# Smaller loads, full-height exponent products and another order of the first steps in a gated recurrence that feeds a mixture of experts

## The chip, the cores and the metric

The kernel runs on one core of a Trainium2 chip. The time is device microseconds of one execution; a kernel's time is the median of its runs. Five engines work side by side, each in the order of its own queue: PE (matrix products; PEld are its weight loads), VectorE (DVE), ScalarE (ACT), GpSimd (POOL) and SyncE (SP, which issues most transfers). [...]

## The reference

A recurrence over 768 positions for 4 batches and 8 heads of width 40, then a two-level choice of one of 16 experts for each of the 3072 tokens:

```python
for t in range(S):
    m_new = np.maximum(f_gate[:, :, t] + m, i_gate[:, :, t])
    f_stab = np.exp(f_gate[:, :, t] + m - m_new)
    i_stab = np.exp(i_gate[:, :, t] - m_new)
    C = f_stab * C + i_stab * np.einsum('bhd,bhe->bhde', vt, kt)
    n = f_stab * n + i_stab * kt
    h_tilde = np.einsum('bhde,bhe->bhd', C, qt)
    denom = np.maximum(np.abs(np.einsum('bhd,bhd->bh', n, qt)), 1.0)
    y[:, :, t] = sigmoid(o_gate[:, :, t]) * h_tilde / denom
x = y.transpose(0, 2, 1, 3).reshape(B * S, H * D)
...
g, e = best group of x, best expert in it
out = g_w * e_w * (relu(x @ w1[g, e]) @ w2[g, e])
```

## The kernel before

The positions are cut into 6 chunks of 128, each of two halves of 64 (`sub`); the batches into 2 groups of two (`bp`). A pair p is chunk c = p // 2 and group g = p % 2, so there are 12 pairs. Inside a chunk the recurrence is written as a masked product, between chunks as a carried state. The stages of a pair are functions:

- `load_qk`, `load_nt`: transfers of keys and queries (two of 320 KB, 40 rows each) and of keys, values and output gates in natural order (one of 968 KB, 128 rows of 7744 bytes). There are two `qk` buffers and three `nt` buffers.
- `exponents` (PE) adds up the exponents of the decays in PSUM: a mask, 16 products with the running sums `Z[:, 0]` and 8 with the sources `Z[:, 1]`, each for one half of the rows. `decays` (ACT) takes their exponential into `ab`. `Z` holds the sums of the gates split into three bf16 parts, one below the other.
- `scores` (PE) multiplies keys and queries, `masked` (DVE) multiplies scores and decays, `values` (PE) multiplies the result with the values.
- `keyw` (POOL) weights the keys, `state` (PE) forms the new state, `decayed` (POOL) and `added` (DVE) carry it on in `Cs`. `carried` (PE) is the queries' product with the carried state, in two groups; `carried2` (DVE) scales each group in `acc`.
- `gate` (ACT), `normed` (DVE) and `rows` (POOL) make the pair's output rows `x`; `store_rows` writes them to DRAM (`x_d`), `turn_rows` (PE transposes, ACT copies) turns them for `logits`, whose routing goes on as a chore.

`step(p)` writes down the work around pair p: values of p, exponents of p + 2, carried of p + 1, state and scores of p + 2. A chore is a list of small operations, mostly DVE's; `go_on(n)` issues n of them, and `STEPS` says how many at the four places of a step. The first chore, `far`, is the gates of chunks 2 to 5: five scans and sums on DVE (`gate_sums`), then the split (`parts`) on ACT and, before, POOL. `near` is the same for chunk 1. `gate_scales` makes the scale factors of a range of chunks.

The program is written under a manual schedule, so every engine's queue has the order of the code. The last products of `values` read a window of 64 columns that reaches into the gate columns of `nt`, so they wait for `gate` of the same pair. After the recurrence come 16 experts; their weights come through SP's queue too.

Of the kernel before, what the change touches and what calls it, by code (L numbers as in the profile page):

```python
# [66 lines left out]
def lstm_moe(ctx: ExitStack, tc: tile.TileContext, gates, qkT, nat, wcat, w1, w2, cst, out):  # L67
# [19 lines left out]
    ind_b, sel_b, hp_b = (cb[0:KP, a:b] for a, b in ((C_IND, C_SEL), (C_SEL, C_HP), (C_HP, C_LT)))  # L87
# [33 lines left out]
    Z = ap_.tile([KP, 2, S], BF16, name="Z")  # L121
    wk = att_pool("wk", 2)
# [49 lines left out]
    def exponents(p):  # L172
# [4 lines left out]
        for hp in range(2):  # L177
            for pr in range(4):
                for bp in range(2):
                    k = (2 * g + bp) * H + 4 * hp + pr  # L180
                    mm(t[SUB * bp:SUB * bp + SUB, hp, pr * P:(pr + 1) * P], bc(ind_b[:, k:k + 1], (KP, SUB)),
                       Z[:, 0, c * P:(c + 1) * P], start=False, stop=False, skip_group_check=True)
        for hp in range(2):
            for sub in range(2):
                for bp in range(2):
                    k = (2 * g + bp) * H + 4 * hp
                    at = c * P + sub * SUB
                    o = t[SUB * bp:SUB * bp + SUB, hp, :].rearrange("p (a s t) -> p a s t", a=4, s=2)[:, :, sub, :]
                    mm(o, Z[:, 1, at:at + SUB], bc(ind_b[:, k:k + 4].unsqueeze(2), (KP, 4, SUB)),  # L189
                       start=False, stop=(sub == 1), skip_group_check=True)  # L190
# [16 lines left out]
    def masked(p):  # L207
        pt = st_[p]["pt"] = wk.tile([P, 2 * H * SUB], F32, name="pt")
# [730 lines left out]
    STEPS = {8: (3, 5, 4, 5), 9: (6, 3, 2, 3), 10: (3, 5, 5, 6)}  # L939
# [19 lines left out]
    def step(p):  # L959
        n = STEPS.get(p) or (3, 4, 2, 3)  # L960
# [3 lines left out]
        run(values, p)  # L964
        run(normed, p)
        run(rows, p)
        if p > -2:
            run(load_nt, p + 3)
# [8 lines left out]
        if turned:  # L977
            logits()
# [418 lines left out]
```

## Time and profile before

| | us |
|---|---|
| median of 3 runs | 428.08 (420.79, 428.08, 431.43) |
| the profiled execution | 421.98 |
| its span | 420.3 |
| PE busy in the span | 374.1 (89%) |
| DVE, ACT, POOL busy | 296.7, 215.7, 134.1 |
| mean granted clock | 0.888 |

The span runs from the first to the last instruction; 1.7 us of the profiled execution lie outside it. Busy shares are means over stages with different limits, so the stages are read one by one below. "Idle before" is the time an engine stood still before an instruction, with what released it.

### The profile page before, as it was taken

To read this page: it belongs to the slowest core of one execution; us is meant where nothing else is said; L and a number is where in the kernel's file an instruction comes from. 1 tells how busy PE (TensorE), PEld (TensorE's weight loads), DVE (VectorE), ACT (ScalarE), POOL (GpSimd) and SP (SyncE) were. 2 spreads that over 40 slices of the span, in tenths; PEclk is the share of its full clock that TensorE was granted. 3 is DMA by queue.
4 is the path that set the end of the run, shared out by engine and by line. 5 is a ranking of instruction groups with operands and counts; after the bars stand their busy time and mean duration, and the time that the engine had idled before them with its cause. 6 is when DMAs were issued, how large, how long until landed. Compare 5 with 4: busy or idle time off the path is not lost.

```text
span 420.3 us, 12565 instructions
## 1 busy us (share of the span) xinstructions
PE 374.1 (89%) x5259; PEld 331.4 (79%) x5259; DVE 296.7 (71%) x695; ACT 215.7 (51%) x419; POOL 134.1 (32%) x143
## 2 busy tenths in 40 slices
PE   8497599779777867699999999999999999999994
PEld 4286377657666756696899999999999999999994
DVE  5457235766658755925788987987987779989893
ACT  2202523322313221445447776666777668888782
POOL 2234433433424233003252227314312343234121
PEclk9855656997969875689999999999999999999998
DMA  7735245674615773421587578568466865688200
GB/s 218 234 80 188 68 131 188 223 245 153 205 61 198 241 264 108 175 110 52 193 317 262 224 252 305 187 255 311 175 230 269 299 236 203 243 301 282 84 17 16
DMA packets 15772, 81.96 MB, mean 195 GB/s; under 512 B 2624, under 2 KB 6438, under 8 KB 11170
## 3 DMA queue, kind: packets, MB, share of 16 engines
q1 hardware_dynamic: 11890, 68.34, 47.3%
q0 software_dynamic: 3600, 12.39, 8.4%
q8 instruction: 42, 0.69, 0.7%
q10 hardware_dynamic: 224, 0.41, 0.3%
q14 instruction: 16, 0.13, 0.1%
HBM read 71.69 MB, written 9.93 MB: 194 GB/s over the span
## 4 chain that ended last, share of the span: by engine, by line
PE 66%; DVE 13%; issue 10%; DMA 4%; POOL 3%; ACT 3%; POOLq 1%; SPq 1%; DVEq 0%; ACTq 0%
PE psh L778 18%; PE po L828 5%; PE po L829 4%; PE po L830 4%; PE sp L204 4%; PE acc L289 4%; DMA nt<-in_nat_dram 4%; PE acc L265 4%; PE tp L332 3%; PE sp L230 3%; PE po L706 2%; PE psh L690 2%; PE po L834 2%; PE lg L353 2%; PE psh L803 2%
## 5 line engine op out<-in xcount | busy, mean ns | idle before, releaser
L608 POOL DMA_INDIRECT out_dram<-y,ix x32 | 36.7, 1146 | 112.9 <-ACT y L842 84.4
L778 PE MATMUL psh<-xhl,w1h 128*128 128x256 f32 (+4 forms) x336 | 58.5, 304 | 0.2
L828 PE MATMUL po<-w2h,hh 128*128 128x320 f32 (+1 forms) x176 | 55.6, 316 | 0.0
L830 PE MATMUL po<-w2h,hh 128*128 128x320 f32 (+1 forms) x176 | 54.4, 309 | 0.0
L829 PE MATMUL po<-w2l,hh 128*128 128x320 f32 (+1 forms) x176 | 54.3, 309 | 0.0
L749 DVE TENSOR_TENSOR w2l<-w2s,w2h 128x640 fp32r<-128x640 f32 x60 | 47.8, 823 | 6.4 <-ACT w2h L745 5.7
L778 PEld LDWEIGHTS psh<-xhl,w1h 128*128 128x128 f32 x336 | 49.8, 188 | 2.0 <-DVE xhl L811 0.6
L778 PE MATMUL psh<-xhl,w1l 128*128 128x128 f32 (+6 forms) x256 | 47.6, 268 | 0.0
L778 PE MATMUL psh<-xhl,wsk 128*128 128x256 f32 (+4 forms) x168 | 47.6, 322 | 0.0
L604 POOL DMA_INDIRECT xg<-x_d,ix x32 | 35.9, 1123 | 31.7 <-DVE hh L880 14.4
L778 PEld LDWEIGHTS psh<-xhl,w1l 128*128 128x128 f32 x256 | 42.3, 189 | 0.4
L749 DVE TENSOR_TENSOR w1l<-w1s,w1h 128x1024 fp32r<-128x1024 f32 x32 | 39.0, 1222 | 4.2 <-ACT w1h L745 4.0
L745 ACT CAST w2h<-w2s 128x640 fp32r<-128x640 f32 x60 | 41.5, 726 | 0.0
L194 ACT ACTIVATE ab<-sp 128x1024 f32<-128x1024 f32 x12 | 12.3, 1024 | 45.7 <-PE sp L189 34.7
L745 ACT CAST w1h<-w1s 128x1024 fp32r<-128x1024 f32 x32 | 33.3, 1046 | 0.0
L828 PEld LDWEIGHTS po<-w2h,hh 128*128 128x128 f32 (+1 forms) x176 | 32.6, 185 | 0.3
L830 PEld LDWEIGHTS po<-w2h,hh 128*128 128x128 f32 (+1 forms) x176 | 32.6, 185 | 0.2 <-DVE hh L880 0.2
L829 PEld LDWEIGHTS po<-w2l,hh 128*128 128x128 f32 (+1 forms) x176 | 32.6, 185 | 0.0
L265 PE MATMUL acc<-Cs,qk 40*64 40x64 f32 x704 | 21.6, 256 | 11.8 <-DVE acc L277 8.4
L334 ACT COPY xT<-tp 128x256 f32<-128x256 f32 x24 | 8.9, 373 | 45.0 <-PE tp L332 30.9
L265 PEld LDWEIGHTS acc<-Cs,qk 40*64 40x64 f32 x704 | 17.2, 163 | 16.1 <-DVE acc L277 9.7
L312 POOL TENSOR_TENSOR x<-sr,den 128x640 f32<-128x640 f32 (+1 forms) x12 | 15.4, 1283 | 44.9 <-DVE den L305 26.6
(208 smaller groups left out, 810.7 us busy)
## 6 DMA issues: line engine op xcount, KB each, us to landing
w1s<-in_w_dram SPq DMA_DIRECT2D x12, 1536.0 KB
w2s<-in_w_dram SPq DMA_DIRECT2D x14, 1280.0 KB
nt<-in_nat_dram SPq DMA_DIRECT2D x12, 968.0 KB
qk<-in_qkT_dram SPq DMA_DIRECT2D x24, 320.0 KB
x_d<-x SPq DMA_DIRECT2D x12, 384.0 KB
w1s<-in_w_dram SPq DMA_DIRECT2D x4, 768.0 KB
w1s<-in_w_dram POOLq DMA_DIRECT2D x2, 1536.0 KB, 7.4
w2s<-in_w_dram SPq DMA_DIRECT2D x4, 640.0 KB
```

What stands on the lines that cost most here:

```text
L204: mm(t[SUB * bp:SUB * bp + SUB, hp, pr * P + SUB * sub:pr * P + SUB * sub + SUB], qk[r, bp, 0, pr, s], qk[r, bp, 1, pr, s], start=True, st ...
L265: mm(acc[SUB * sub:SUB * sub + SUB, bp, 2 * pr + hp, :], qk[r, bp, 1, pr, SUB * sub:SUB * sub + SUB], Cs[r, at:at + WIN], start=(swap == 0 ...
L289: mm(acc[SUB * sub:SUB * sub + SUB, bp, j, :], pt[r, k:k + SUB], nt[r, v:v + WIN], start=(c == 0 and sub == 0 and j == 0), stop=(j == H - ...
L312: (e or nc.gpsimd).tensor_tensor(t["x"][:, bs, 0:DM].rearrange("p b (h d) -> p b h d", d=D), t["sr"][:, hs].rearrange("p (b h) d -> p b h ...
L604: return nc.gpsimd.indirect_dma_start(out=o, out_offset=None, in_=src, in_offset=bass.IndirectOffsetOnAxis(ap=idx, axis=0))
L608: return nc.gpsimd.indirect_dma_start(out=out, out_offset=bass.IndirectOffsetOnAxis(ap=idx, axis=0), in_=y, in_offset=None, bounds_check=N ...
L745: nc.scalar.copy(t[names[0]][:, dst], src[r][:, s])
L749: nc.vector.tensor_tensor(o, src[r][rows, s], h.bitcast(F32), op=ALU.subtract)
L778: mm(ps[:, g, 0:n_], w[:, s], x, start=(part == 0 and n == 0), stop=(part == 1 and n == len(todo[1]) - 1), skip_group_check=True)
L828: mm(po[0:m], hh[:, f, t], w2h[:, s], start=st0, stop=False)
L829: mm(po[0:m], hh[:, f, t], w2l[:, s], start=False, stop=False)
L830: mm(po[0:m], hh[:, f, tl], w2h[:, s], start=False, stop=sp0)
```

## The change

Four things change. A pair's `qk` load becomes 8 transfers (2 KB a row) and its `nt` load 6 (1296 or 1280 bytes a row). `exponents` uses full-height products: 8 with a table `ind2`, built once, and 4 with `zb`, the sources of both batches, which POOL's new stage `sources` makes a step ahead. `masked` writes over `ab`. And the order changes: pair 0's carried products, scales and `values` stand before pair 1's state, with 13 filler products (`busy`) between them; `keyw` of pair 1 stands behind `decayed` of pair 0; the chore `far` is spread over steps 0 and 1 behind the scalings, and its subtractions are on DVE; `turn_rows` of a pair's second half moves to the next step, between the two groups of `carried`, and `logits` behind `store_rows`.

```diff
@@ load_qk, load_nt
         for hp in range(2):
-            nc.sync.dma_start(qk[64 * hp:64 * hp + D], qkT[c, g, D * hp:D * hp + D])
+            for bp in range(2):
+                for i in range(2):
+                    nc.sync.dma_start(qk[64 * hp:64 * hp + D, bp, i], qkT[c, g, D * hp:D * hp + D, bp, i])
...
-        nc.sync.dma_start(nt, nat[c, g])
+        for a, b in ((0, NV // 2), (NV // 2, NV), (NV, NV + NV // 2), (NV + NV // 2, NTW), (NTW, NTW + DM), (NTW + DM, NTW + 2 * DM)):
+            nc.sync.dma_start(nt[:, a:b], nat[c, g, :, a:b])
@@ exponents
             for pr in range(4):
-                for bp in range(2):
-                    k = (2 * g + bp) * H + 4 * hp + pr
-                    mm(t[SUB * bp:SUB * bp + SUB, hp, pr * P:(pr + 1) * P], bc(ind_b[:, k:k + 1], (KP, SUB)),
-                       Z[:, 0, c * P:(c + 1) * P], start=False, stop=False, skip_group_check=True)
+                mm(t[:, hp, pr * P:(pr + 1) * P], ind2[:, g * H + 4 * hp + pr, :], Z[:, 0, c * P:(c + 1) * P],
+                   start=False, stop=False, skip_group_check=True)
         for hp in range(2):
             for sub in range(2):
-                for bp in range(2):
-                    k = (2 * g + bp) * H + 4 * hp
-                    at = c * P + sub * SUB
-                    o = t[SUB * bp:SUB * bp + SUB, hp, :].rearrange("p (a s t) -> p a s t", a=4, s=2)[:, :, sub, :]
-                    mm(o, Z[:, 1, at:at + SUB], bc(ind_b[:, k:k + 4].unsqueeze(2), (KP, 4, SUB)),
-                       start=False, stop=(sub == 1), skip_group_check=True)
+                o = t[:, hp, :].rearrange("p (a s t) -> p a s t", a=4, s=2)[:, :, sub, :]
+                mm(o, st_[p]["zb"][:, sub].rearrange("k b s -> k (b s)"), bc(hd_b[:, 4 * hp:4 * hp + 4].unsqueeze(2), (KP, 4, SUB)),
+                   start=False, stop=(sub == 1), skip_group_check=True)
+
+    def sources(p):
+        c, g = divmod(p, 2)
+        z = st_.setdefault(p, {})["zb"] = wk.tile([KP, 2, 2, SUB], BF16, name="zb")
+        nc.gpsimd.tensor_tensor(z, bc(Z[:, 1, c * P:(c + 1) * P].rearrange("k (s t) -> k s t", s=2).unsqueeze(2), (KP, 2, 2, SUB)),
+                                bc(b_b[:, 2 * g:2 * g + 2].unsqueeze(1).unsqueeze(3), (KP, 2, 2, SUB)), op=ALU.mult)
@@ masked
-        pt = st_[p]["pt"] = wk.tile([P, 2 * H * SUB], F32, name="pt")
+        pt = st_[p]["pt"] = st_[p]["ab"]
@@ step
-    STEPS = {8: (3, 5, 4, 5), 9: (6, 3, 2, 3), 10: (3, 5, 5, 6)}
+    STEPS = {0: (0, 3, 1, 1), 1: (0, 2, 1, 1), 8: (3, 4, 7, 6), 9: (6, 3, 2, 3), 10: (3, 5, 5, 6)}
...
-        n = STEPS.get(p) or (3, 4, 2, 3)
+        n = STEPS.get(p) or (3, 5, 3, 4)
...
         run(carried, p + 1, 0)
-        if turned:
-            logits()
+        if p > 0:
+            turn_rows(2 * p - 1)
         run(carried2, p + 1, 0)
...
+        listed()
+        store_rows(p)
+        run(load_qk, p + 3)
+        if turned:
+            logits()
+        turn_rows(2 * p)
...
-        if p >= 0:
-            turn_rows(2 * p + 1)
...
+        run(sources, p + 3)
@@ before the first step
-        near, far = gates_of(1, 2), gates_of(2, NCH, nc.scalar.copy, nc.gpsimd)
+        near, far = gates_of(1, 2), gates_of(2, NCH, nc.scalar.copy)
...
         steps(near, 2)
-        keyw(1)
+        spare = ps_1.tile([P, 4, P], F32, name="tp", tag="lg")
+        busy(4, spare)
         state(0)
         added(0, 0)
         decayed(0, 1)
+        keyw(1)
+        busy(3, spare)
         carried(0, 0)
+        busy(2, spare)
         carried2(0, 0)
-        steps(near, 2)
+        carried(0, 1)
+        busy(2, spare)
+        carried2(0, 1)
+        gate(0)
+        added(0, 1)
+        load_qk(2)
+        values(0)
+        busy(2, spare)
         state(1)
...
+        decayed(1, 1)
+        scores(1)
         steps(near, 99)
...
         for p in range(2):
-            step(p)
+            step(p, p == 0)
```

POOL's queue around pair 1's keys, before (`nt` with buffer numbers is the product `keyw`, `Cs` is `decayed`, `x` is `rows`, `Zr` the subtractions of `far`):

```order
L218 TENSOR_TENSOR nt_109<-nt_109,ab_107 128x2x320
L218 TENSOR_TENSOR nt_110<-nt_110,ab_108 128x2x320
L241 TENSOR_TENSOR Cs<-Cs,decs 128x328 x2
L312 TENSOR_TENSOR x<-sr,den 128x2x320
L218 TENSOR_TENSOR nt_111<-nt_111,ab_107 128x2x320
L241 TENSOR_TENSOR Cs<-Cs,decs 128x328
L1105 TENSOR_TENSOR Zr<-AC,Z 32x2x512
L1109 TENSOR_TENSOR Zr<-Zr,Zm 32x2x512
```

The same stretch of POOL's queue after:

```order
L194 TENSOR_TENSOR zb<-Z,cb 96x256 x2
L223 TENSOR_TENSOR nt_110<-nt_110,ab_108 128x2x320
L246 TENSOR_TENSOR Cs<-Cs,decs 128x328
L223 TENSOR_TENSOR nt_111<-nt_111,ab_109 128x2x320
L246 TENSOR_TENSOR Cs<-Cs,decs 128x328
L194 TENSOR_TENSOR zb<-Z,cb 96x256
L317 TENSOR_TENSOR x<-sr,den 128x2x320
L223 TENSOR_TENSOR nt_112<-nt_112,ab_108 128x2x320
```

`decayed` of pair 0 moved ahead of the keys of pair 1, the two subtractions left the queue, and `zb` came in.

DVE's queue in step 0, before, from the end of pair 0's normalising (`M_`, `Dl` and `AC` of 512 columns are `far`, `acc` is `carried2`, `pt` is `masked`):

```order
L305 RECIPROCAL den<-den 128x16
L1087 SCALAR_TENSOR_TENSOR M__122<-G,M__122 32x512
L1090 TENSOR_TENSOR Dl<-G,M__122 32x512
L1092 TENSOR_TENSOR Dl<-Dl,M__122 32x512
L277 TENSOR_TENSOR acc<-acc,eacol 64x2x4x41
L209 TENSOR_TENSOR pt<-sp,ab_108 128x1024
L277 TENSOR_TENSOR acc<-acc,eacol 64x2x4x41
L1094 SCALAR_TENSOR_TENSOR AC<-R__125,Dl 32x512
```

The same stretch of DVE's queue after:

```order
L310 RECIPROCAL den<-den 128x16
L282 TENSOR_TENSOR acc<-acc,eacol 64x2x4x41
L214 TENSOR_TENSOR ab_109<-sp,ab_109 128x1024
L282 TENSOR_TENSOR acc<-acc,eacol 64x2x4x41
L1094 SCALAR_TENSOR_TENSOR M__123<-G,M__123 32x512
L1097 TENSOR_TENSOR Dl<-G,M__123 32x512
L1099 TENSOR_TENSOR Dl<-Dl,M__123 32x512
L254 TENSOR_TENSOR Cs<-Cs,sp 128x328
```

The two scalings and the masked product of pair 1 moved ahead of the far gates.

PE's queue in step 3, before, from the carried products on (`tp` are the transposes of `turn_rows`, L230 is `state`, L204 is `scores`):

```order
L265 MATMUL acc<-Cs,qk_104 64x64 x32
L332 MATMUL tp<-cs,x 128x128 x2
L332 MATMUL tp<-cs,x 64x128
L230 MATMUL sp<-nt_111 64x41 x32
L332 MATMUL tp<-cs,x 128x128 x2
L332 MATMUL tp<-cs,x 64x128
L204 MATMUL sp<-qk_105 64x64 x32
```

The same stretch of PE's queue after:

```order
L270 MATMUL acc<-Cs,qk_105 64x64 x16
L337 MATMUL tp<-cs,x 128x128 x2
L337 MATMUL tp<-cs,x 64x128
L270 MATMUL acc<-Cs,qk_105 64x64 x16
L337 MATMUL tp<-cs,x 128x128 x2
L337 MATMUL tp<-cs,x 64x128
L235 MATMUL sp<-nt_112 64x41 x32
L209 MATMUL sp<-qk_106 64x64 x32
```

One group of transposes moved from behind `state` to between the two carried groups, a step later.

## Rows read from the trace of the kernel before

**Rows 1.** Stages: busy us of each engine, granted clock, DMA share, GB/s.

```profile
0.00:20.00 20.00, 13.73 (x223) 7.59 (x223) 9.73 (x31) 4.48 (x8) 4.01 (x8) 0.97 0.80 234
26.50:47.60 21.10, 13.85 (x317) 11.15 (x316) 11.41 (x15) 7.37 (x12) 9.42 (x6) 0.58 0.40 122
47.60:60.60 13.00, 11.79 (x238) 8.99 (x238) 5.04 (x13) 3.68 (x11) 5.09 (x10) 0.50 0.50 159
60.60:168.00 107.40, 87.28 (x2576) 69.32 (x2576) 67.44 (x212) 28.57 (x71) 38.57 (x50) 0.80 0.55 184
210.00:420.00 210.00, 204.36 (x1460) 197.60 (x1458) 174.07 (x332) 149.57 (x264) 67.20 (x59) 1.00 0.62 224
```

**Rows 2.** Chain of waits to 60 us: start, us, what.

```profile
3.90 15.62 DMA nt<-in_nat_dram
...
19.66 1.33 POOL nt L218
...
21.03 1.95 PE sp L230 x64
...
39.23 1.05 ACT Z L1104
...
40.36 2.13 POOL Zr L1105
...
46.84 0.74 ACT nt L170
...
47.63 0.48 PE acc L289 x4
...
53.74 0.83 PE tp L332 x3
```

**Rows 3.** PE's waits from 60.6 to 168 us: total, times, longest.

```profile
PE acc L265 <- DVE acc L277: 5.2, 4, 3.0
PE sp L230 <- issue: 2.7, 1, 2.7
...
PE tp L332 <- DVE hi__71 L439: 1.9, 2, 0.9
...
PE tp L332 <- ACT xT L335: 0.5, 1, 0.5
```

**Rows 4.** Timeline of the first 8 us: start, us, engine, line, operation.

```profile
0.87 0.72 SPq L1137 DMA_DIRECT2D G<-in_gates_dram  x1
...
1.65 0.99 SPq L159 DMA_DIRECT2D qk<-in_qkT_dram  x2
...
4.00 0.41 DVE L1087 TENSOR_TENSOR_SCAN M__122<-G 32x128 f32<-32x128 f32 x1 [1.89 <-DMA G<-in_gates_dram]
...
5.41 0.25 DVE L1096 TENSOR_TENSOR AC<-G,M__122 32x128 f32<-32x128 f32 x1
...
7.09 0.41 DVE L1109 TENSOR_TENSOR Zr<-Zr,Zm 32x256 f32<-32x256 f32 x1
```

**Rows 5.** DMA queues up to 26.5 us: packets, MB, share (q1 SP's, q10 ACT's).

```profile
q1 hardware_dynamic: 739, 4.54, 59.3%
q10 hardware_dynamic: 224, 0.41, 5.5%
```

**Rows 6.** Stage of the far gates on DVE, columns as in rows 1.

```profile
29.70:39.20 9.50, 6.91 (x124) 5.60 (x120) 9.27 (x10) 1.74 (x4) 4.50 (x3) 0.50 0.59 190
```

**Rows 7.** Timeline of PE's exponents at the half clock.

```profile
97.99 1.03 PE L176 MATMUL sp<-cb 128*128 128x512 bf16 x2
...
98.96 1.06 PE L181 MATMUL sp<-Z,cb 96*64 96x128 bf16 x16
...
99.81 0.97 PE L189 MATMUL sp<-cb,Z 96*64 96x256 bf16 x8
```

**Rows 8.** Two stretches around a stall, columns as in rows 1.

```profile
114.00:116.00 2.00, 0.07 (x4) 0.00 (x0) 0.30 (x2) 0.09 (x1) 0.00 (x0) 1.00 0.70 211
...
118.00:120.00 2.00, 1.81 (x39) 1.46 (x43) 1.93 (x8) 0.85 (x3) 0.78 (x1) 0.50 0.12 25
```

More of the change, by code (lines that the diff above doesn't have):

```diff
@@ L86, in lstm_moe @@
     ident_b, later_b = cb[:, C_ID:C_ID + P], cb[:, C_M2:C_M2 + SUB]
[L87 removed]
+    ind_b, sel_b, hp_b, hd_b, b_b = (cb[0:KP, a:b] for a, b in ((C_IND, C_SEL), (C_SEL, C_HP), (C_HP, C_HD), (C_HD, C_B), (C_B, C_LT)))
     wc = const.tile([P, 3, 32], F32, name="wc")
@@ L957, in run, with step @@
             stage(p, *a)
-    def step(p):
-        n = STEPS.get(p) or (3, 4, 2, 3)
+    def step(p, begun=False):
+        n = STEPS.get(p) or (3, 5, 3, 4)
         turned = p % 2 == 0 and 0 < p < NP
@@ L963, in step @@
             last_rows()
[L964 to L968, printed above, removed]
+        if not begun:
+            values(p)
+        normed(p)
+        rows(p)
+        run(load_nt, p + 3)
         run(exponents, p + 2)
@@ L984, in step @@
         run(carried2, p + 1, 1)
-        if p >= 0:
-            store_rows(p)
-            if p > -1:
-                run(load_qk, p + 3)
-            turn_rows(2 * p)
+        listed()
[4 more added lines that the diff above has]
+        turn_rows(2 * p)
         if p == NP - 3:
@@ L992, in step @@
             assert not marks
+        go_on(n[1])
+        run(state, p + 2)
         if turned:
             chores.append(turned_logits(p // 2 - 1))
-        go_on(n[1])
-        run(state, p + 2)
         run(added, p + 2, 0)
@@ L1005, in step @@
         run(scores, p + 2)
+        run(sources, p + 3)
         if p == 3:
             first_rows()
-        listed()
         go_on(n[3])
@@ L1012, in step @@
         if p == NP - 3:
+            listing(ps_1.tile([P, 4, P], F32, name="tp", tag="tp"))
+            listed()
             rt["early"] = select(top[:, 0, :], nc.vector)
@@ L1042, in last_pairs @@
         xl = early_turn((0, 0), EARLY, xgs[0], ((ps_s, "sp"), (ps_s, "sp")))
+        turn_rows(2 * p - 1)
         values(p)
@@ L1149, in lstm_moe @@
         nc.gpsimd.tensor_copy(cb, cs[:, 0:C_LT])
+        for bp in range(2):
+            (nc.scalar.copy, nc.gpsimd.tensor_copy)[bp](
+                ind2[:, :, SUB * bp:SUB * bp + SUB].rearrange("k (g h) s -> k g h s", g=2),
+                bc(ind_b.rearrange("k (g b h) -> k g b h", g=2, b=2)[:, :, bp, :].unsqueeze(3), (KP, 2, H, SUB)))
         for p in range(3):
@@ L1154, in lstm_moe @@
         steps(gates_of(0, 1), 99)
-        near, far = gates_of(1, 2), gates_of(2, NCH, nc.scalar.copy, nc.gpsimd)
+        near, far = gates_of(1, 2), gates_of(2, NCH, nc.scalar.copy)
+        sources(0)
         exponents(0)
@@ L1158, in lstm_moe @@
         scores(0)
+        sources(1)
         gate_scales(0, 1)
         keyw(0)
-        steps(near, 3)
+        steps(near, 2)
         exponents(1)
@@ L1169, in lstm_moe @@
         decayed(0, 1)
+        keyw(1)
+        busy(3, spare)
         carried(0, 0)
+        busy(2, spare)
         carried2(0, 0)
-        steps(near, 2)
+        carried(0, 1)
[6 more added lines that the diff above has]
+        busy(2, spare)
         state(1)
-        added(0, 1)
         added(1, 0)
-        carried(0, 1)
-        carried2(0, 1)
-        load_qk(2)
+        decayed(1, 1)
+        scores(1)
         steps(near, 99)
-        gate(0)
-        decayed(1, 1)
+        sources(2)
+        gate_scales(1, 2)
         added(1, 1)
-        scores(1)
-        gate_scales(1, 2)
         nc.sync.dma_start(wc, wcat)
@@ L1364, in _lay @@
         cst[:KP, C_HP + i] = at % H // 4 == i
+    for i in range(H):
+        cst[:KP, C_HD + i] = at % H == i
+    for i in range(B):
+        cst[:KP, C_B + i] = at // H == i
     cst[:, C_LT:C_LT + P] = np.triu(np.ones((P, P)), 1)
```

6 lines of the change are left out of this document (3 added, 3 removed).

## The prediction

> **What bounds the kernel now.** I read the stage table first. [...] There the two first steps stand out: step 0 takes 21.1 us and step 1 takes 13.0, at a granted clock of 0.58 and 0.50, while the 107.4 us after them hold nine steps, about 12 us each [rows 1]. Next I read the chain of waits for these two steps. It begins with a transfer: pair 1's keys and values, issued at 3.90, are first used by POOL at 19.66 [rows 2]. Later it runs through the three-way split of the far gates, ACT's casts and POOL's subtractions in turn (1.05 and 2.13 us apiece, from 39.23 on), and then ACT's gate of pair 1 at 46.84, queued behind them; the last four products of `values` of pair 1 wait for that gate until 47.63 [rows 2]. For the later steps I read what PE waited for: 5.2 us for VectorE's (DVE's) scaling of `acc`, 6.6 us in all for the turned rows (seven waits; the row shown first is the largest group, the last the smallest), and 6.2 us in three groups that no record explains ("issue", the longest 2.7) [rows 3].
>
> **The change part by part.**
>
> Loads in pieces. A pair's load is 14 transfers from SP's queue in place of 3. Two issues took 0.99 us [rows 4], so 0.5 us each: 14 and the store take 7.5 us of a 12 us step, in a queue that has room. In the build a transfer also waits for the one issued eight places earlier. Pair 1's last piece is SP's 29th issue: at 0.5 us it goes out by 15.7, and the first gate load, issued at 0.87 for 0.72 us and used at 4.00, shows 2.4 us to landing [rows 4], so 18.1: not later than the landing of today, 19.5. Bytes of short rows are not dear: up to 26.5 us the SP loads (7.7 to 8.2 KB a row) move 4.54 MB with 59.3% of the engines, 0.0766 MB for each per cent; ACT's (1.9 and 2.6 KB) 0.41 MB with 5.5%, 0.0745 [rows 5]. That is 3% a byte. POOL's product with the keys needs only the first three of six pieces, so 0.5 MB less; at 234 GB/s [rows 1] that is 2.1 us. Ends for the keys: 17.4 and 20.0 (3% and one issue on top of today's 19.5); I take 18.5, between them and nearer the first, since the bytes are what the row shows.
>
> [...]
>
> Before step 0. POOL's `decayed` of pair 0 no longer queues behind the product that waits for pair 1's keys; carried, scaled and `values` of pair 0 run while they are still on their way, with 13 filler products. So PE's `values` of pair 0 (64 records, like the state's 1.95 us [rows 2]) leave the stretch after the landing. After it now: POOL 1.33 to 19.8, PE's state of pair 1 1.95 to 21.8, DVE's copy of 328 columns 0.5 (an estimate from 0.41 for 256 [rows 4]), then what is left of chunk 1's gates on DVE. The same operations took 2.4 us for chunk 0 (from 5.41 to 7.50, and one cast of 0.3 more [rows 4]): 24.7. Here the change is dearer: those gates now stand behind the state, and POOL's new `sources` follows: 256 columns, at the 1.33 us of 640 columns [rows 2] 0.5, and twice that if the broadcast operands slow it; I take 0.6. Step 0's exponents have their operands at about 25.3, and DVE is free for step 0. Before, DVE had normalised pair 0 and begun the far gates at 29.7 [rows 6].
>
> Steps 0 and 1. DVE was busy 11.41 + 5.04 = 16.5 us in them [rows 1]. It takes over POOL's two subtractions: 0.41 us for 256 columns [rows 4], four times as wide, 1.6 each, so 19.7. [...] DVE's 9.27 us between 29.7 and 39.2 [rows 6] hold some 7 us of the far gates, all ahead of or between the scalings that `values` of pair 1 needs; now these scalings come first and the split falls behind step 1's. What is late next is DVE itself: in order, it still waits for ACT's casts twice (1.05 us each), for POOL's decay once (328 columns at the rate above, 0.7) and for a carried group on PE once (half of the 64 products of 1.95 us, 1.0), estimates from [rows 2]: 19.7 + 3.8 = 23.5 us, above PE's 22.8. With slack for the hand-overs 25 us: step 2 starts at 50.3 where it started at 60.6. **Gain 10 us**; ends 7 (DVE at the contended prices and PE's work in line with it) and 13 (23 us, keys at 17.4).
>
> Exponents. The two groups of part-height products took 0.85 us from start to start (98.96, 99.81) and 0.97 in all at the low clock, and the two full products of 512 columns before them 0.97 (97.99 to 98.96) [rows 7]. The 8 and 4 new ones stream 1024 columns a group at full height, so 0.97 each: two half-height ones shared the array already. That is 0.1 us dearer a pair at the low clock; if their starts are the bound, half as many gain 0.9. I take 0, nearer the column count. It drops 12 products and their weight loads a pair.
>
> Turned rows. `turn_rows(2p-1)` now stands between the two carried groups, where PE waits for DVE: 5.2 us of waits, of which the longest, 3.0, is a queue of chores on DVE that three transposes (0.83 us [rows 2]) only shorten. I count 3. Its own waits for `listed` (6.6 us) stay in the odd steps, as turn_rows(2p) now waits for it there (about 0.9 in each of four), and hide behind the logits in the even ones: 3 more. `masked` in place adds no wait: the exponents of the pair that reuse the buffer already stand behind `values`. `sources` is 0.6 us on POOL, which is busy 38.57 of 107.4 [rows 1], and is used a step later; if that cover were gone it would add 0.6 a step. Of the unexplained 6.2 us I count none: the longest falls where the transfers run at a share of 0.70 (PE 0.07 us busy from 114 to 116 [rows 8]), and neither shorter rows nor fewer instructions is shown to cure them. **Gain 6 us**, ends 0 (DVE, 67 of 107 us busy, is late next each time) and 12 (the stalls go too).
>
> Sum: 421.98 - 10 - 6 = 406 for an execution like the profiled one. The median of the three runs is 6.1 us above that one, and I carry this over: **412 us**.
>
> **The rivals.** (a) More than that: the stalls and what they cost go. After the one at 114 the clock falls from 1.00 to 0.50 by 118 [rows 8], where PE's work takes twice as long: 1.81 us in the two shown, 0.9 lost, and some 3 over six us. All 6.2 us and two such stretches make 12 more than the 406: 394 as profiled, 400 as the median. For: eight places in flight hold fewer bytes in front of whatever PE waits for. Against: no row names that cause. [...] (c) Slower: SP's queue becomes the bound. Fourteen issues and a store outlast a 12 us step from 0.8 us apiece on, if the wait for the eighth transfer before, which lands only after the queue's other bytes, paces them. At 1.0 us nine steps take 15 us, 135 in place of 107.4, 28 more; with the 10 gained ahead of them, 446. For: each load now waits for another's landing ahead of it in the same queue. Against: eight pieces are at least 0.65 MB, 2.8 us at 234 GB/s, longer than the 2.4 to land, so the queue keeps the engines fed. [...] (d) The products don't get fewer in time at all, as costed: no change of the sum.
>
> **How the numbers follow.** Forecast 0.58 (404 to 419), (a) 0.16 (396 to 404), (b) 0.20 (419.5 to 430), (c) 0.06. The runs before spread from 420.79 to 431.43, so 2% is about what a measurement of this kernel can tell from no change. Faster by over 2% (below 419.5): 0.58 + 0.16 = 0.74; same 0.20; slower 0.06. The range leaves out half of (a), most of (c) and the upper part of (b): 401 to 424.
>
> **What would show it.** The profile of the changed kernel should show: POOL's product of pair 1 at 17.4 to 20; `values` of pair 0 before 20; the gates' ACT casts after 38 and `values` of pair 1 without a wait for ACT; step 2's `values` at 48 to 53; PE's wait for the scaling of `acc` below 3 us; the stretch from the end of the last step to the end unchanged. Keys after 21, SP issues over 0.8 us apart in the steps, or step 2 at 57 and later would make it wrong.

## The result, and the profile after

The changed kernel takes 409.86 us in the median of four runs (410.01, 417.18, 409.70, 408.52); the kernel before took 425.88 beside it. The ratio is 0.970, interval 0.961 to 0.979: faster, at the predicted place (412, range 401 to 424). Its profiled execution is 410.01 us with a span of 408.3, against 421.98 and 420.3. Some executions are slower, at a lower clock: the medians and ranges below include them, the ratios leave them out, and the traces of `half_height`, `choice_later` and `both_moves_half_height` show such an execution, so that I read from them only what does not hang on the clock.

The stages of the changed kernel, with the columns of [rows 1]: the first 20 us (step 0 begins at 18.20 in them), step 0, step 1, steps 2 to 7, step 8, steps 9 and 10, the expert part. A step is counted from the first product of `values` of its pair to that of the next. The granted clock is a share of the full one; in this trace and in that of the kernel before it is recorded as 1.00 or 0.50 alone, and a number between them is the mean of a stretch.

```profile
0.00:20.00 20.00, 18.26 (x304) 10.32 (x304) 10.46 (x27) 6.00 (x9) 8.07 (x12) 1.00 0.74 216
18.20:36.00 17.80, 13.68 (x374) 11.01 (x378) 10.99 (x23) 3.17 (x8) 6.02 (x7) 0.70 0.67 210
36.00:50.70 14.70, 9.53 (x294) 7.56 (x286) 9.69 (x19) 7.64 (x15) 7.10 (x11) 0.85 0.48 148
50.70:114.70 64.00, 53.06 (x1781) 43.26 (x1782) 42.15 (x123) 20.54 (x49) 29.52 (x41) 0.93 0.66 202
114.70:132.10 17.40, 12.65 (x300) 9.89 (x295) 11.45 (x45) 3.64 (x9) 5.51 (x10) 0.68 0.48 141
132.10:158.40 26.30, 20.38 (x454) 16.44 (x446) 15.35 (x50) 7.41 (x17) 7.58 (x11) 0.69 0.61 206
200.00:408.00 208.00, 201.48 (x1442) 194.97 (x1441) 171.28 (x323) 148.98 (x263) 66.95 (x58) 0.99 0.62 225
```

Step 2 starts at 50.70 in place of 60.56, and pair 11's `values` at 158.38 in place of 169.97; from there to the end both kernels take the same (249.9 and 250.3 us), with PE busy 201.48 of 208 us at a clock of 0.99 here and about as much before (last line of [rows 1]): that part is PE's own work, and the end moves with the end of step 10. So of the 12.0 us of the span 9.9 come ahead of step 2 and only 1.7 in steps 2 to 10. Within those steps the lead grew to 17.6 us at pair 8 (114.73 against 132.33), and step 8, 17.4 us in place of 11.1, gave 6.3 of it back. Half of these 6.3 go with the clock: PE was busy 12.65 us in step 8, at a granted clock of 0.68, and 9.40 before, at 0.92, for about as many products (300 and 302 records). Step 8 of the kernel before:

```profile
132.30:143.40 11.10, 9.40 (x302) 7.66 (x305) 8.97 (x37) 3.55 (x10) 3.92 (x7) 0.92 0.54 190
```

POOL around pair 1's keys, and PE's exponents of pair 2 at the low clock (the rows that answer to [rows 2] and [rows 7]):

```profile
18.13 1.29 POOL L223 TENSOR_TENSOR nt<-nt,ab 128x640 f32<-128x640 f32 x1 [1.86 <-DMA nt<-in_nat_dram]
...
25.67 0.61 POOL L194 TENSOR_TENSOR zb<-Z,cb 96x256 bf16<-96x256 bf16 x1 [2.16 <-DVE Z L1118]
```

```profile
27.09 1.06 PE L183 MATMUL sp<-Z,ind 96*128 96x128 bf16 x8
27.94 1.06 PE L188 MATMUL sp<-cb,zb 96*128 96x256 bf16 x4
28.93 1.12 PE L270 MATMUL acc<-Cs,qk 40*64 40x64 f32 x16
```

The keys are used at 18.13 (18.5 predicted), `sources` takes 0.61 us (0.6), and the exponents take 0.85 and 0.99 us from start to start where the half-height ones, twice as many of the same number of columns, took 0.85 and 0.97. At a clock of 1.00 the first group takes 0.45 us here (75.41 to 75.86), about half.

PE's waits in steps 2 to 10, total, times, longest, to be held against [rows 3]:

```profile
PE lg L402 <- DVE oh L397: 5.9, 5, 1.8
PE acc L270 <- DVE sr L308: 3.3, 2, 1.9
PE acc L294 <- issue: 3.0, 2, 1.5
PE tp L1133 <- ACT eacol L1126: 2.9, 1, 2.9
PE tp L506 <- POOL mark L499: 2.0, 1, 2.0
PE tp L337 <- DVE lists L512: 1.8, 2, 0.9
PE acc L270 <- DVE acc L282: 1.2, 3, 0.6
PE sp L209 <- issue: 1.1, 2, 0.8
PE tp L337 <- DVE sg L425: 1.1, 1, 1.1
PE sp L180 <- DVE Cs L254: 1.1, 1, 1.1
PE tp L337 <- POOL Cs L246: 0.8, 1, 0.8
PE sp L188 <- issue: 0.4, 1, 0.4
```

The wait for the scaling of `acc` fell from 5.2 to 1.2 us, the turned rows' (L337, L332 before) from 6.6 to 3.7. But the largest is new: the products that rank the tokens (L402) wait 5.9 us for DVE's one-hot `oh`; before they waited 0.3. The wait for `sr`, the last reader of `acc`, went from 1.3 to 3.3, and the ones for `mark` and for `Cs` (2.0 and 1.1) are new. The waits without a releaser ("issue") fell from 6.2 to 4.5. So 8.6 us of waits went and 10.7 came; that the steps are 1.7 us shorter all the same goes with PE's clock, 0.83 in them in place of 0.80. (The wait of L1133 for `eacol` ends at 50.45 and belongs to step 1.)

**The stalls with no cause in the records.** PE's two long ones in this stretch stand at 72.5 and 93.8; this is the end of the first. Beside it PE's instruction queue, q8, with the packet that starts between 71.6 and 71.7 us (packets, MB, share: all of the packet's 1.01 us is counted against this 0.1 us of 16 engines, hence 63.4%), and the same queue's line for the whole span:

```profile
72.14 0.33 PE L294 MATMUL acc<-nt,ab 64*64 64x64 f32 x7
73.99 1.04 PE L294 MATMUL acc<-nt,ab 64*64 64x64 f32 x54 [1.52 <-issue]
```

```profile
q8 instruction: 1, 0.02, 63.4%
```

```profile
q8 instruction: 41, 0.67, 0.7%
```

I counted PE's instructions (products, weight loads and the waits of its queue) up to each such stall. In all fourteen traces, up to 172 us, the place of each such stall over 0.3 us is 193 plus a multiple of 256 (the product itself, or the weight load just ahead of it), and the stalled instruction starts 1.2 to 1.9 us after the end of a packet of q8, whose size is 0.67 MB / 41, or 16.4 KB: here the packet starts at 71.65, takes 1.01 us and PE goes on at 73.99. So these are waits for the next block of PE's own program: in this trace PE's queue has 10,410 instructions, 10,256 of them products and weight loads, and q8 41 packets, 254 instructions to a packet, which fits the 256 between two such places. I call such a place a block's edge. The longest wait at one was 3.4 us in the kernels with the loads cut by columns or whole, and 5.5 us with the loads cut by rows.

### The profile page after: what moved, and what is told of

It reads as the page before. It is cut to its first block, busy times and chain, and to the rows that moved or that the text cites. A ratio compares the mean times of both kernels' runs of the same rounds, so it can differ in the third digit from the quotient of the medians.

```text
span 408.3 us, 12562 instructions
## 1 busy us (share of the span) xinstructions
PE 366.5 (90%) x5128; PEld 325.3 (80%) x5128; DVE 297.5 (73%) x697; ACT 216.5 (53%) x420; POOL 137.8 (34%) x154
## 4 chain that ended last, share of the span: by engine, by line
PE 62%; DVE 16%; issue 11%; DMA 3%; POOL 2%; ACT 2%; SPq 1%; POOLq 1%; DVEq 0%; ACTq 0%
PE psh L783 19%; PE po L833 5%; PE po L835 5%; PE po L834 5%; PE acc L270 3%; PE sp L235 3%; PE acc L294 2%; PE po L711 2%; PE tp L337 2%; PE psh L695 2%; PE sp L142 2%; PE po L839 2%; PE psh L808 2%; PE po L838 1%; PE lg L358 1%
## 5 line engine op out<-in xcount | busy, mean ns | idle before, releaser
L613 POOL DMA_INDIRECT out_dram<-y,ix x32 | 38.0, 1187 | 112.8 <-ACT y L847 84.3
L199 ACT ACTIVATE ab<-sp 128x1024 f32<-128x1024 f32 x12 | 12.3, 1024 | 49.7 <-PE sp L188 49.7
L783 PEld LDWEIGHTS psh<-xhl,wsk 128*128 128x128 f32 x168 | 29.5, 190 | 0.1
L894 ACT COPY hs<-psh 128x320 f32<-128x320 f32 (+3 forms) x40 | 17.3, 434 | 16.5 <-PE psh L783 14.0
L895 DVE TENSOR_TENSOR hs<-hs,psh 128x320 f32<-128x320 f32 (+3 forms) x40 | 19.8, 496 | 8.6 <-ACT hs L894 8.3
L317 POOL TENSOR_TENSOR x<-sr,den 128x640 f32<-128x640 f32 (+1 forms) x12 | 14.6, 1219 | 33.0 <-DVE den L310 16.5
```

Of the source, the lines that this page charges most:

```text
L199: nc.scalar.activation(ab, st_[p]["X"].rearrange("p r n -> p (r n)"), AF.Exp)
L317: (e or nc.gpsimd).tensor_tensor(t["x"][:, bs, 0:DM].rearrange("p b (h d) -> p b h d", d=D), t["sr"][:, hs].rearrange("p (b h) d -> p b h ...
L613: return nc.gpsimd.indirect_dma_start(out=out, out_offset=bass.IndirectOffsetOnAxis(ap=idx, axis=0), in_=y, in_offset=None, bounds_check=N ...
L783: mm(ps[:, g, 0:n_], w[:, s], x, start=(part == 0 and n == 0), stop=(part == 1 and n == len(todo[1]) - 1), skip_group_check=True)
L894: nc.scalar.copy(src[p], ps[:, :, W:2 * W])
L895: nc.vector.tensor_tensor(src[p], src[p], ps[:, :, 0:W], op=ALU.add)
```

## The experiments

Twelve kernels ran; the table has six of them beside the kernel before and the changed one, the others have their numbers under their headings. It gives the start of `values` of pairs 2 and 11 and what lies between them (us, profiled execution), PE's longest stall at a block's edge up to 172 us, the number of blocks whose packet started over 2.5 us after the edge before (of those with a packet behind it), the median and range of the runs, and the ratio to the kernel before with its interval.

| kernel | pair 2 | pair 11 | between | longest | late blocks | median (range) | ratio |
|---|---|---|---|---|---|---|---|
| before | 60.56 | 169.97 | 109.4 | 2.7 | 8 of 23 | | |
| changed | 50.70 | 158.38 | 107.7 | 1.5 | 2 of 27 | 409.86 (408.5 to 417.2) | 0.970 (0.961 to 0.979) |
| changed_again | 50.57 | 159.36 | 108.8 | 1.5 | 1 of 27 | 411.27 (409.8 to 415.7) | 0.980 (0.968 to 0.991) |
| old_turns | 49.70 | 157.07 | 107.4 | 1.8 | 5 of 27 | 415.70 (408.7 to 417.9) | 0.982 (0.974 to 0.989) |
| first_steps_alone | 55.82 | 167.32 | 111.5 | 3.4 | 10 of 25 | 419.19 (415.8 to 425.1) | 0.987 (0.981 to 0.993) |
| whole_loads | 51.58 | 164.49 | 112.9 | 2.8 | 7 of 26 | 419.19 (413.6 to 426.9) | 0.983 (0.977 to 0.988) |
| pieces_alone | 59.61 | 166.74 | 107.1 | 1.7 | 3 of 27 | 419.94 (418.7 to 426.3) | 0.988 (0.984 to 0.992) |
| rank_later_choice_later | 52.09 | 153.65 | 101.6 | 1.5 | 3 of 27 | 408.84 (405.3 to 411.6) | 0.972 (0.963 to 0.982) |

The ratio of one and the same kernel came out as 0.970 and 0.980, so two kernels less than 1% apart are not told from each other here. Single traces spread more: steps 2 to 10 have the same order in the changed kernel, in its second trace, in `blocks_shifted` and in `no_filler` (below), and took 107.7, 108.8, 110.4 and 114.4 us. A difference of under 7 us between two traces in these steps is not told from that.

**1. The old order of the turned rows.** In the changed kernel:

```diff
-        if p > 0:
-            turn_rows(2 * p - 1)
+        if turned:
+            logits()
...
+        if p >= 0:
+            turn_rows(2 * p + 1)
         go_on(n[2])
```

with the counts of the kernel before, 8: (3, 5, 4, 5) and (3, 4, 2, 3).

> The changed kernel with the turned rows, the logits and the routing chores at their old places in the step and in the old counts; loads, exponents and first steps stay changed. Theory: the new order of the turned rows gained some 7.7 us up to step 7 and lost 6.3 of them again in step 8, because it brings a late routing chain and full DVE queue with it. Then steps 2 to 10 take 109.4 us again as in the kernel before (values of pair 2 at 50.7, of pair 11 at 160, in place of 158.4), the time is 411 to 413 us, and the wait of the rank products for DVE's one-hot (5.9 us) is gone while the turned rows wait for listed again (about 6 us). Rival: step 8's loss has nothing to do with the turned rows (the clock and the choice of experts on DVE alone): then it comes on top, values of pair 11 at 164 to 167, time 416 to 419.

Steps 2 to 10 took 107.4 us, not 109.4, and the new order 107.7 and 108.8: by the traces no gain of it can be seen. Step 8 took 10.9 us, so its loss belongs to the new order, as the theory had it; but steps 9 and 10 took 30.2 us there and 26.2 with the new order, so that little of it is kept to pair 11. L402 waited 0.3 us, and the turned rows waited again: 1.9, 1.9, 1.1, 0.9 and 0.5 us. But the lead up to pair 7 was there without the new order (55.6 us from pair 2 to pair 7, and 55.1 with it; 60.8 before). That half of my theory fell. The interval of the ratio overlaps the changed kernel's two: the times don't tell the two orders apart.

**2. The new first steps alone**, in the kernel before: the order of the prologue, `step(p, p == 0)`, counts 0: (0, 3, 1, 1) and 1: (0, 2, 1, 1), and `gates_of(2, NCH, nc.scalar.copy)`; loads, exponents and turned rows stay.

> The kernel before with the new order of the first steps alone (prologue with filler products, step 0 begun early, far gates spread behind the scalings, their subtractions on DVE); whole loads, half-height exponents and old turned rows stay. Theory: this order is nearly all of the first term, so values of pair 2 start at 50.5 to 52 (60.6 before, 50.7 with everything) and the time is 414 to 416.5 us, 0.975 of the kernel before. Rival: it needs the pieces and the exponents to pay: values of pair 2 at 54 to 57, 419 to 422 us.

Step 2 started at 55.82 and the time was 419.19: the rival's time, 1.3% below before. The trace says where most of the other 5 us were: PE stopped for 1.94 us among the carried products of pair 0, at a block's edge, and the clock was at 0.56 in the 2 us from 18 on, which is 1.00 in the changed kernel. `values` of pair 0 took 1.99 us in place of 1.16 and started 3.4 us later, and step 0 took 19.3 us in place of 17.8. Pair 1's keys were not late, though the loads are whole: they were used at 18.79. A second such stop, 3.38 us, came in step 1 and cost little: that step took 14.9 us in place of 14.7, as pair 2's first products wait for ACT there anyway (0.56 us behind the stop, 2.9 in the changed kernel).

```profile
18.06 0.59 PE L265 MATMUL acc<-Cs,qk 40*64 40x64 f32 x8 [1.94 <-issue]
...
51.37 0.33 PE L230 MATMUL sp<-nt 64*64 64x41 f32 x2 [3.38 <-issue]
```

```profile
18.79 1.29 POOL L218 TENSOR_TENSOR nt<-nt,ab 128x640 f32<-128x640 f32 x1 [2.32 <-DMA nt<-in_nat_dram]
```

```profile
18.00:20.00 2.00, 1.94 (x18) 0.99 (x19) 0.52 (x1) 0.00 (x0) 1.21 (x1) 0.56 0.66 272
```

**3. Whole loads**, in the changed kernel:

```diff
-            for bp in range(2):
-                for i in range(2):
-                    nc.sync.dma_start(qk[64 * hp:64 * hp + D, bp, i], qkT[c, g, D * hp:D * hp + D, bp, i])
+            nc.sync.dma_start(qk[64 * hp:64 * hp + D], qkT[c, g, D * hp:D * hp + D])
...
-        for a, b in ((0, NV // 2), (NV // 2, NV), (NV, NV + NV // 2), ...):
-            nc.sync.dma_start(nt[:, a:b], nat[c, g, :, a:b])
+        nc.sync.dma_start(nt, nat[c, g])
```

> The changed kernel with a pair's load in 3 transfers again. Theory: the pieces only bring pair 1's keys forward, by about 1 us: product of pair 1 with its keys on POOL at 19.0 to 20.0 us in place of 18.13, values of pair 2 0.5 to 1.5 us later (51.2 to 52.2), steps 2 to 10 unchanged, 410 to 412 us. Rival 1: the pieces also keep the queue's other loads out of PE's way, so the unexplained stalls grow from 4.5 back to 6 us and more: 413 to 416. Rival 2: 14 issues a pair cost something somewhere: under 409.

Pair 1's keys were used at 20.34, 2.2 us later and a little later than expected, and step 2 started 0.9 us later, as expected. Steps 2 to 10 took 112.9 us, 4 to 5 more than in the changed kernel's two traces, which is within the spread of traces named above. Rival 1 was the nearer one, in its direction: PE's stalls without a releaser in these steps are 6.7 us in place of 4.5 and 3.8, the longest is 2.8 us, and 7 blocks come late. The ratio, 0.983, lies above the changed kernel's 0.970 and 0.980, but the intervals overlap: what the pieces are worth inside the changed kernel isn't told by the times.

**4. Half-height exponents**, in the changed kernel: the 24 old products of `exponents` in place of the 12; `ind2` and `sources` left out.

> The changed kernel with the old 24 half-height products of the exponents, without the table and without the sources on POOL. Theory: columns set the time, two half-height products share the array, so the exponents take the same 0.85 and 0.97 us at the low clock and 0.45 each at the full one; POOL gets 0.6 us a pair back, and time is 409 to 411 us. Rival: 12 more products and weight loads a pair cost 0.5 to 0.9 us a pair, 5 to 9 us over the steps: 415 to 419.

408.65 us (404.58 to 414.86), ratio 0.960 (0.951 to 0.970): not slower. The rival is out; whether the old form is a little faster can't be told from these runs.

**5. The pieces cut by rows**, in the changed kernel:

```diff
-            for bp in range(2):
-                for i in range(2):
-                    nc.sync.dma_start(qk[64 * hp:64 * hp + D, bp, i], qkT[c, g, D * hp:D * hp + D, bp, i])
+            for a, b in ((0, 16), (16, 32), (32, D)):
+                nc.sync.dma_start(qk[64 * hp + a:64 * hp + b], qkT[c, g, D * hp + a:D * hp + b])
...
+        for a in range(0, P, 16):
+            nc.sync.dma_start(nt[a:a + 16], nat[c, g, a:a + 16])
```

> The changed kernel with a pair's load still in 14 transfers, but cut the other way: 16 (or 8) whole rows of 7.7 to 8 KB each instead of all rows in pieces of up to 2 KB. In the traces so far every unexplained stall of PE falls on an instruction whose place in PE's own stream is 193 plus a multiple of 256, and ends 1.2 to 1.6 us after a 16,384-byte packet of PE's instruction queue. From the boundary before to that packet the kernels with whole loads take 2.2 to 2.9 us in the mean (8 to 12 of some 27 over 2.5 us), those with pieces 1.3 to 1.9 (2 to 6 over 2.5 us). Theory: the instruction packets wait behind long rows, so the length of a row decides: 2.2 us and more in the mean, 8 or more over 2.5 us, 415 to 420 us. Rival: the number of bytes under way decides, which 14 transfers through eight places limit however they are cut: 1.3 to 1.9 us, 2 to 6 over 2.5 us, 409 to 412 us.

The delays quoted there count every packet; with the first packet behind each edge alone, as in the table, they are 1.9 to 2.2 us in the mean and 7 to 10 late ones with long rows, 1.1 to 1.6 and 1 to 5 with pieces. 441.27 us (439.99 to 442.28), ratio 1.048 (1.040 to 1.056): 14 transfers a pair, and slower than 3. The packets came 2.3 us after the edge in the mean, 10 of 23 over 2.5. PE's waits from 20 to 163 us, the longest three groups of stalls:

```profile
PE sp L208 <- issue: 13.3, 4, 5.5
PE acc L293 <- issue: 6.6, 3, 4.8
...
PE sp L182 <- issue: 2.7, 1, 2.7
```

So the number of transfers under way is not what helps. The time is 21 us above the theory's end, and the loads themselves got dearer: from 60 to 150 us queue 1 moved 13.84 MB with 84.1% of the engines' time, 6.1% a MB, and in the changed kernel's second trace 16.87 MB with 60.4%, 3.6% a MB. It is not the rows' length that makes the bytes dear: with whole loads the same long rows cost 3.4% a MB. Pair 1's keys were used at 28.51. So this kernel changes two things, the rows' length and what a byte costs, and how much of the stalls each makes isn't told apart. These lines are the queue's in the three traces, cut by rows, the changed kernel's second, whole loads:

```profile
q1 hardware_dynamic: 5079, 13.84, 84.1%
```

```profile
q1 hardware_dynamic: 10988, 16.87, 60.4%
```

```profile
q1 hardware_dynamic: 4664, 16.96, 57.4%
```

**6. The changed kernel again**, without an edit.

> The changed kernel itself once more, for a second trace and more times beside the others. If the loss in step 8 (17.4 us from values to values where the kernel before took 11.1) is made by the order, it comes again: 15 us or more, with the 1.8 us wait of the rank products and normalising that starts over 2 us after values end. If it is the clock of one execution, step 8 takes 11 to 13 us and another step is long instead. Time 408 to 414 us.

Step 8 took 17.0 us again, with the same waits. It is made by the order. DVE's rows at the end of step 7, PE's two waits, and DVE's first operation of `first_experts` and of `normed` in the kernel before:

```profile
116.24 0.49 DVE L254 TENSOR_TENSOR Cs<-Cs,sp 128x328 f32<-128x328 f32 x1
...
118.92 0.17 DVE L306 TENSOR_SCALAR den<-acc 128x16 f32<-128x16 f32 x1
119.22 0.82 DVE L308 SCALAR_TENSOR_TENSOR sr<-nt,acc 128x640 f32<-128x640 f32 x1
```

```profile
120.19 1.39 PE L270 MATMUL acc<-Cs,qk 40*64 40x64 f32 x32 [1.68 <-DVE sr L308]
...
129.92 0.21 PE L402 MATMUL lg<-oh,lt_b 128*128 128x64 bf16 x1 [1.79 <-DVE oh L397]
```

```profile
132.19 0.17 DVE L527 SCALAR_TENSOR_TENSOR key<-cntf,keyb 128x16 f32<-128x16 f32 x1
...
133.96 0.17 DVE L301 TENSOR_SCALAR den<-acc 128x16 f32<-128x16 f32 x1
```

`values` of pair 8 end at 117.1, but nine operations of `first_experts` (L532 to L550) stand ahead of `normed`, which starts at 118.92; the carried products wait for it. The same nine stood there before, too. But before they began at 132.19, as pair 8's `values` did (132.33), and `normed` followed 0.4 us after the end of `values`; now DVE comes to them only as `values` end, behind the operations of the routing that start later in the new order. PE was busy 0.52 of the 2 us from 118 to 120; from 120 to 132 the clock is 0.51.

**7. Both moves**, in the changed kernel:

```diff
-    STEPS = {..., 8: (3, 4, 7, 6), ...}
-    ASIDE = {7: 9, 8: 9}
+    STEPS = {..., 2: (3, 5, 3, 3), 4: (3, 5, 3, 3), 6: (3, 5, 3, 3), 8: (3, 4, 5, 8), ...}
+    ASIDE = {7: 0, 8: 9}
...
         run(carried2, p + 1, 1)
+        if p == 8:
+            aside(9)
```

> The changed kernel with two counts moved: one routing operation fewer in steps 2, 4 and 6, so that the rank products stand behind the next step's exponents, and 5 and 8 instead of 7 and 6 in step 8; and the choice of experts out of step 7's end into the middle and the end of step 8. Theory: PE's wait for the one-hot (5.9 us, five times) falls to 2 us (step 10's stays) and step 8 takes 11 to 13 us, so 404 to 408 us. Rival: DVE is late whatever stands first, and the waits come back under other names or as a low clock: 409 to 413 us.

The median is 408.84 us, just behind the expected 404 to 408, the span 403.6 in place of 408.3 and 408.1, and steps 2 to 10 took 101.6 us, 6 to 7 less. L402 waits 1.7 us in all, step 2 takes 9.4 in place of 12.6 and step 8 13.7. The same places as above:

```profile
116.13 0.17 DVE L306 TENSOR_SCALAR den<-acc 128x16 f32<-128x16 f32 x1
```

```profile
PE lg L402 <- DVE oh L397: 1.7, 1, 1.7
```

It is the best trace of all: its steps 2 to 10 are 6.1 us below the shortest of the four with the unmoved order. By the times it can't be told from the changed kernel (0.972 and, beside it, 0.980, with overlapping intervals).

**8. No filler products**, in the changed kernel: `spare` and the five lines `busy(4, spare)` to `busy(2, spare)` left out.

> The changed kernel without the 13 filler products before and behind the carried products of pair 0. Theory: they keep PE busy until pair 1's keys have landed; without them PE stands still at 13 to 18 us and the clock falls to 0.50 before 20 us (1.00 until 25 with them), values of pair 0 take 1.9 us instead of 1.16, and values of pair 2 start 1 to 2 us later, at 51.7 to 52.7: 411 to 414 us. Rival: the clock falls at 25 us in any case and nothing is lost: values of pair 2 at 50 to 51, 409 to 411 us.

The first half of the theory held (the granted clock is 0.78 from 18 to 20 us and 0.50 from 20 on), the second fell: step 2 started at 50.11, not later. In these steps PE's clock is not what is late. The times (411.09 to 424.56, median 416.20) overlap the changed kernel's and give no ratio; the trace loses in steps 4 and 6 (15.4 and 16.8 us), whose order is the changed kernel's, and why is open.

**9. The pieces alone**, in the kernel before: only `load_qk` and `load_nt` as in the change.

> The kernel before with a pair's load in the 14 pieces of up to 2 KB a row, and nothing else changed. Theory: the pieces pay by themselves, because PE's instruction packets no longer wait behind long rows: 1.1 to 1.9 us from one boundary to the next packet in the mean (2.9 in the kernel before), at most 6 of 27 over 2.5 us, and 4 to 6 us less, ratio 0.985 to 0.991. Pair 1's keys come at 18 to 19 us, yet values of pair 2 still start after 58.5. Rival: they pay only through pair 1's keys in the new order: no difference that can be told, ratio 0.994 to 1.003.

419.94 us, ratio 0.988 (0.984 to 0.992), as the theory had it. Pair 1's keys are used at 18.70, step 2 starts at 59.61, the packets come 1.3 us after the edge in the mean (3 of 27 late), and the clock stays at 1.00 from 70 to 110 us, where the kernel before has 0.69 from 90 to 100. By the traces 1.0 us of the gain lies ahead of step 2 and 2.3 in steps 2 to 10, the latter within the spread of traces.

**10. PE's program shifted**, in the changed kernel:

```diff
-        busy(24)
+        busy(10)
+        tiny = pair_banks()
+        for _ in range(64):
+            mm(tiny[:, 0, 0:4], ones_b, ones_b[:, 0:4], start=True, stop=True)
```

> The changed kernel with 10 of the 24 starting products of 512 columns and 64 products of 4 columns in place of the other 14, so that PE's program holds 50 products more ahead of everything and takes about as long there. Theory: the stalls belong to places in PE's stream of instructions; they still fall on instructions 193 plus a multiple of 256, which are now other products of the recurrence: none of the long ones stays on the products that it struck in the changed kernel (12 to 13 products into the state of pair 1, 37 into the scores of pair 3, 10 into the values of pair 4, 46 into those of pair 6). Their sum stays between 4 and 10 us, the time 408 to 414 us. Rival: they belong to the operations (a bank, a semaphore, a late transfer that the records do not show) and strike the same products again.

The stalls moved. They stand again on instructions 193 plus a multiple of 256, and these are now others. First the changed kernel's second trace, then the shifted one:

```profile
46.36 0.68 PE L209 MATMUL sp<-qk 40*64 40x64 f32 x27 [1.53 <-issue]
...
72.36 1.04 PE L294 MATMUL acc<-nt,ab 64*64 64x64 f32 x54 [1.26 <-issue]
...
94.81 0.50 PE L294 MATMUL acc<-nt,ab 64*64 64x64 f32 x18 [1.52 <-issue]
```

```profile
47.18 0.37 PE L235 MATMUL sp<-nt 64*64 64x41 f32 x10 [0.61 <-issue]
...
96.65 0.27 PE L209 MATMUL sp<-qk 40*64 40x64 f32 x2 [1.15 <-issue]
109.11 0.38 PE L294 MATMUL acc<-nt,ab 64*64 64x64 f32 x4 [0.89 <-issue]
```

The one in the scores of pair 3 is now in the state ahead of them, the one in pair 6's `values` in the scores ahead of those. The rival is out. The sum, 3.8 us, is just under the expected 4 to 10. The time, 415.19 us (ratio 0.978, 0.973 to 0.983), is above the expected 408 to 414; step 2 starts 2.5 us later, at 53.22, behind the tiny products.

**11. The choice of experts later**, alone: of experiment 7 only `ASIDE` and `aside(9)`.

> The changed kernel with the choice of experts alone moved out of step 7's end into step 8; the routing counts stay. Theory: normalising of pair 8 starts as soon as its values end, the 1.9 us wait of the carried products for it goes, and step 8 takes 14 to 15.5 us (17.4 and 17.0 with the change, 13.7 with both moves); step 2 stays at 12.2 to 12.6, as it has the wait for the one-hot (9.4 with both moves): 409 to 411.5 us. Rival: step 8 needs the routing counts: still 16.5 us or more.

Step 8 took 14.6 us, as expected: 2.4 to 2.8 less than in the changed kernel, where it had lost some 6. So the place of the choice is part of step 8's loss and not the whole of it; with both moves, too, 13.7 us are left against 11.1 before. The wait for the one-hot stayed (5.7 us, five times). Step 2 took 15.1 us where 12.2 to 12.6 were expected, at a granted clock of 0.50 (0.77 in the changed kernel), and is not read. The median is 413.16 (405.06 to 418.06), the ratio 0.959 (0.952 to 0.966): the two point apart, and I take no time from it.

**12. Both moves with half-height exponents.**

> The changed kernel with both moves (rank products later, choice of experts later) and the old half-height exponents, so without the table and without the sources on POOL. Theory: the height of the products makes no difference, and the time is that of the two moves: 404 to 410 us, ratio 0.960 to 0.972. Rival 1: the half-height form is faster by itself, as its median beside the changed kernel's could mean: under 404 us. Rival 2: it costs where the clock is full: over 411 us.

408.61 us (405.79 to 413.44), ratio 0.960 (0.953 to 0.967): the expected case, no difference from the full-height form of experiment 7 that the intervals separate. But `half_height`, without the moves, has the same ratio, 0.960, beside its own runs of the kernel before: what the two moves gain in the trace of experiment 7 no time shows.

## Why the prediction was right, and where it was not

**The first term was right, with most of its steps.** Step 2 at 50.70 (50.3 predicted), keys at 18.13, the gates of chunk 1 used from 25.6 (25.3), `values` of pair 0 from 18.20, ACT's casts of the far split from 43.60 (after 38), PE's wait for the scalings under 3 us. That the 25 us from there to step 2 came out is luck in part: DVE was busy 17.3 us in them and not 19.7, and the waits were 8.1 us where I had 3.8 and 1.5 of slack. PE's 22.8 us, which the prediction sets beside DVE's 23.5, are its busy 25.6 us in the two steps of [rows 1] less 1.95 and 0.83; it was busy 18.9. At the end the split was late, ACT's last cast of it at 48.25 for 1.04 us, and PE waited 2.9 us for ACT:

```profile
25.30:50.70 25.40, 18.86 (x461) 15.02 (x461) 17.31 (x33) 10.31 (x22) 11.16 (x15) 0.70 0.55 169
```

Alone the order reached 55.8, with everything but the pieces 51.6, with everything but the turned rows 49.7. So alone it gave 4.7 of the 9.9 us, though no other part, taken out of the changed kernel, moves step 2 by more than 1 us. What it lacked alone was time lost at a block's edge (1.94 us) and at the low clock in the prologue (0.56 from 18 to 20 us), not the keys; whole loads had no such stall there in experiment 3, so that this is the long rows' doing is not shown. The fillers, which I had put in the sum only as company, are worth nothing there.

**Exponents: 0 was right**, as were `sources` and SP's queue: the eight issues of a `qk` load took 3.3 to 4.6 us in the steps, 0.41 to 0.57 apiece, so rival (c) had no ground. In the changed kernel's trace the transfers of SP and ACT take eight semaphores in turn and each of SP's waits for the one that it sets, so for the transfer eight places earlier; SP's waits for a landing come to 1.1 us from 50 to 160 us.

**The term "Turned rows, gain 6" failed.** Its two parts came as computed (4.0 and 2.9 us less waiting), and still steps 2 to 10 took 107.7 us, 1.7 less than before, and 107.4 with the old order. I looked only at what `turn_rows` itself waits for. I passed over what the same diff moved with it: the chore of `logits` starts behind `state` instead of ahead of it, so DVE's chain to the one-hot has only the scores to hide behind (5.9 us of waits), and DVE comes later to the choice of experts and to pair 8's normalising behind it; in step 8 the clock fell as well. Moving just the counts and the choice gave 6 to 7 us in the steps in one trace, about the size of the term that I had predicted. The waits that came are shown; that they are the whole of the missing 4 us is not, as one trace of the same steps differs from another by up to 7 and the times show nothing of the moves.

**The step "Of the unexplained 6.2 us I count none" failed too**, the other way. I had said that no row shows shorter rows to cure them. Experiments 3, 9 and 10 show what they are, waits for blocks of PE's program, and that with long rows 7 to 10 blocks come late and with pieces 1 to 5 of 24 to 27 (6 without the fillers). Pieces alone gave 1.2%, about 5 us. So rival (a) held in part, and a small one: in steps 2 to 10 the stalls went from 6.2 us to 4.5 and 3.8 in the changed kernel's two traces and to 4.1 with the pieces alone, and `old_turns`, which has the pieces too, had 7.4. Not all of them go. By an estimate from these traces: the changed kernel's PE uses up a block in as little as 3.6 us, and the packets' 1.2 us delay, 1.0 us and 1.4 us to PE's start make as much, so that a packet that is later still makes PE stand.

**The carried 6.1 us** were not there: the changed kernel's profiled execution is at its median, not below. The sum gave 406 for it and it took 410.0; the two errors cancel, so the 412 is better than its working.

**Open:** how much of the pieces' gain is the stalls and how much the clock that stays up; what the first steps lack without the rest of the change; why 16 long rows a transfer cost 1.7 times the engine time a byte; why traces of the same steps differ by 7 us; and the few us between kernels 4, 7, 11 and 12.

## What to carry to other kernels

A program of many small products can wait for its own next block, as PE did here for up to 5.5 us: where PE stalls without a releaser, count its instructions, and if the stalls lie multiples of one number apart (256 here), try the loads around them in column pieces (here rows of up to 2 KB in place of 8, worth 1.2%). When an operation is moved to hide its wait, follow the whole chain that moves with it, above all the small operations that another engine has to finish before the next product, and place their counts again. A gain that is read from the waits that go is only half a sum: the ones that come must stand beside it. And before a difference between two traces is explained, look how far two traces of the same steps lie apart.

## What the runs showed of the hardware

- PE's stalls without a releaser fall on places a multiple of 256 apart in its stream of instructions and end 1.2 to 1.9 us after a 16.4 KB packet of its instruction queue; a packet takes about 1.0 us and mostly starts 0 to 5 us after the edge before. Over 2.5 us it was for 7 to 10 of some 25 blocks where loads have rows of 8 KB, for 1 to 6 where they are in column pieces.
- From 60 to 150 us the loads' queue took 6.1% of the DMA engines' time a MB with transfers of 16 (or 8) whole rows, 3.6% with column pieces of all rows and 3.4% with whole loads.
- With the filler products left out the granted clock fell some 6 us earlier (0.78 from 18 to 20 us and 0.50 from 20, with them 0.50 from 25.4 on), and step 2 still started no later.
